# A planner with measured costs, and a second bank for the first heads' values, in an attention and two-MoE kernel

## The chip, the cores and the metric

The program runs on one core of one Trainium2 chip. The metric is the device time of one execution in microseconds; the median of the runs shown stands for the kernel. Every engine works through a list of instructions in order; what a list waits for is told by semaphores.

## The reference

Three stages follow each other on 2304 tokens (4 batches of 576) of width 512. First an attention with 8 heads of 64, causal, with a bias made from a running sum of `max(s, 0)`. Then a dense MoE-like layer (512 to 2048 to 512). Then a second one with eight experts (512 to 1024 to 512 each), whose weights per token come from eight rounds of row and column normalisation.

```python
scores = where(causal, -1e9, q @ k.T / 8 + minimum(-(cum_q - cum_k), 0))
attn = softmax(scores) @ v                      # 4 x 8 heads, 576 x 64
h = x @ w_in;  x = (h * sigmoid(1.702 * h)) @ w_out
P = balance(exp(x @ w_gate))                    # 8 rounds
out = sum_e P[:, e] * (relu(x @ w1[e]) @ w2[e])
```

All results are float32, and products are made from split numbers: a matrix product takes three fast ones (high by high, high by low, low by high).

## The kernel before, in words

Each of the 32 heads is handled in two parts, so that there are 64 "heads" in the code: the first 256 query rows (one unit, query blocks 0 and 1), and the other 320 (three units, blocks 2, 3 and 4). Eight parts of one kind make a group; the first group is n = 0 to 7. A unit passes four steps: `scores` (TensorE writes `sp`; VectorE adds the mask and takes the maximum into `sm`, a custom instruction with a read of its accumulator; ScalarE takes the exponential), `turn` (TensorE transposes `sm` into `tp`, which is copied to `pf`, or for n from 14 on split into `ph` and `pl`), `values` (TensorE multiplies with V into the tile `op`) and, when a head is whole, `finish` (VectorE divides: `stats`, reciprocal, `xg`).

PSUM has eight banks. Two hold the scores (tags S0 and S1), two the transposes (T0 and T1), one `op` (tag "O" of the pool `ps_a`), one `hp` (tag "h" of `ps_m`, first product of the first MoE), and two the sums of the first MoE (acc0 and acc1). As there is one bank for `op`, the values of head n wait until `finish` of head n-1 has read it.

The first MoE runs beside the attention, in blocks of 256 tokens and pairs of 128 hidden columns (`mm1`, `mm2`); a block can start when its heads are finished and its rows are transposed (`flush_x`). Its weights come as 64-bit words and are converted on the way (`conv`: two ScalarE passes, one VectorE pass into `t`, a copy to the high half `wih`/`woh`, a subtraction to the low half `wil`/`wol`). The last two blocks run together (`wide1`, `wide2`), and then the second MoE starts with its own planner mode (`seq.fine`).

The order of each engine's list is not written by hand. A `Sequencer` simulates the program while it is built: it gives each operation a cost, a time at which its operands are ready (the end of what it depends on plus a latency), and an end. TensorE's operations are issued at once, and its simulated clock, `free["PE"]`, is the time of the plan; operations of the other engines are held and issued when their simulated time comes, by rank (0 before 1 before 2; weight conversion has 2). The main loop asks in this order: vpow, flush, value, turn, score, first MoE. It takes the first that can start by the plan's time. Where none can, it moves the time itself:

```python
seq.free["PE"] = min(min(times), now + 100)
```

Work that two engines can do is given out by the plan too: `any_copy` takes VectorE or ScalarE, whichever has the lower load, `any_less` VectorE or GpSimd. All engines' rows carry L279, the line that records an operation.

Of the kernel before, what the change touches and what calls it, by code (L numbers as in the profile page):

```python
# [9 lines left out]
F32 = mybir.dt.float32  # L10
F32R = mybir.dt.float32r
# [22 lines left out]
BYTES = {F32: 4, F32R: 4, I32: 4, F16: 2, BF16: 2, U8: 1}  # L34
# [4 lines left out]
N_KF = 4  # L39
ADDING = 3.6  # L40
AFTER_OWN = 34
N_F = 14
NEXT_V = 11
LATE = 3000.0
# [5 lines left out]


class Op:
    __slots__ = ("engine", "call", "cost", "ready", "end", "waits", "after", "rank", "number", "nbytes", "late", "tail")


class Sequencer:
# [10 lines left out]
    def __init__(self):  # L67
        self.free = dict.fromkeys(self.ENGINES, 0.0)
        self.held = {e: [] for e in self.ENGINES}
        self.touched = {}  # L70
        self.earlier = {}
        self.rings = {}
        self.dma = self.issued = 0.0
        self.rank = 0
        self.holding = False
        self.fine = False
        self.late = 0.0
        self.count = 0
        self.outside = set()
# [50 lines left out]
    def cost(self, engine, what, out, ins, sums=False):  # L130
        n = max(self.size(x) for x in [out] + ins[:2])
        psum = any(x.space == PSUM for x in ins)
        if self.fine:
            if engine == "PE":
                return self.size(out) * (4 if ins[0].dtype == F32 else 1) / 2.4 + (13 if ins[0].dtype == F32R else 2.7)
            by = any(self.size(x) == 1 for x in ins[1:]) and n > 1
            if engine == "DVE":
                quick = what in ("tensor_copy", "tensor_scalar") and not psum
                return 66 + 60 * by + n / (1.92 if quick else 0.96)
            if engine == "ACT":  # L140
                return (50 if psum else 90) + 100 * by + 93 * sums + n / 1.2
        if engine == "PE":
            n = self.size(out)
            if what == "transpose":
                return 2 * n / 2.4
            slow = ins[0].dtype == F32 or ins[0].dtype == F32R and n < 256
            return n * (4 if slow else 1) / 2.4
        if engine == "DVE":
            quick = what in ("tensor_copy", "tensor_scalar") and not psum
            return 70 + n / (1.92 if quick else 0.96)  # L150
        if engine == "ACT":
            return 90 + n / 1.2
        return 80 + n * {"memset": 0.3, "tensor_scalar": 2.7}.get(what, 2.24)


    def submit(self, engine, what, call, outs, ins, adds=False):
        op = Op()
        op.engine, op.call, op.end, op.rank, op.number = engine, call, None, self.rank, self.count
        op.ready, op.waits, op.after, op.nbytes, op.tail = 0.0, set(), [], 0, 0
        op.late = self.late + (2000 if self.fine and self.rank else 0)  # L160
        self.count += 1
        if what == "dma_start":
            op.cost = 60 if engine == "SP" else 1000
            op.nbytes = self.size(outs[0]) * outs[0].shape[0] * (2 if self.fine and outs[0].dtype == F16 else 4)
            if adds and self.fine:
                op.nbytes *= ADDING
        else:
            sums = len(outs) > 1
            op.cost = self.cost(engine, what, outs[0], ins, sums) + (190 if sums and not self.fine else 0)
            if self.fine:  # L170
                op.tail = {"DVE": 85, "ACT": 110}.get(engine, 0) + 90 * sums
        for ap, writes in [(x, False) for x in ins] + [(x, True) for x in outs]:
            name = ap.tensor.name
            if name in self.outside:
                continue
            parts, cols = self.where(ap)
            mine = self.touched.setdefault(name, [])
            for x in self.touched.get(self.earlier.get(name), ()):
                self.depend(op, x[3])
            for x in mine:  # L180
                if (writes or x[2]) and x[3] is not op and not (ap.space == DRAM and writes and x[2]):
                    if x[0][0] < parts[1] and parts[0] < x[0][1] and x[1][0] < cols[1] and cols[0] < x[1][1]:
                        self.depend(op, x[3])
            mine[:] = [
                x for x in mine
                if x[3].end is None or x[3].engine != engine or x[2] != writes or x[0] != parts or x[1] != cols
            ]
            mine.append((parts, cols, writes, op))
        if engine == "PE" or not self.holding:
            self.issue(op)  # L190
        else:
            self.held[engine].append(op)

    def depend(self, op, on):
        if on.end is None:
            op.waits.add(on)
            on.after.append(op)
        elif self.fine and on.engine == op.engine != "PE" and not on.nbytes:
            op.ready = max(op.ready, on.end + AFTER_OWN)
        elif on.engine != "PE" or op.engine != "PE":  # L200
            op.ready = max(op.ready, on.end + LATENCY.get((on.engine, op.engine), LATENCY.get(on.engine, 0)))

    def issue(self, op):
        for x in sorted(op.waits, key=lambda x: x.number):
            if x.end is None:
                self.issue(x)
        e = op.engine
        start = max(self.free[e], op.ready)
        self.free[e] = start + op.cost
        op.end = start + op.cost + op.tail  # L210
        if op.nbytes:
            self.issued = max(self.issued, start) + 475
            self.dma = max(self.dma, self.issued + 1200) + op.nbytes / 360
            op.end = self.dma + 440 + op.late
        if op in self.held[e]:
            self.held[e].remove(op)
        op.call()
        op.call = None
        for x in op.after:
            x.waits.discard(op)  # L220
            self.depend(x, op)
        op.after = None

    def when(self, op):

# [95 lines left out]
def kernel(  # L321
# [12 lines left out]
    seq = Sequencer()  # L334
    nc = Core(seq, tc.nc)
    seq.outside |= {x.tensor.name for x in (qk, vP, s, w_in, w_out, wg, w1, w2, out)}
    B, H, D, S = qk.shape[0], qk.shape[1], qk.shape[2] // 2, qk.shape[3] // 2
# [45 lines left out]
    ps_m = Pool(seq, ctx.enter_context(tc.tile_pool(name="ps_m", bufs=1, space=PSUM, reuse_waits="tile")))  # L383
    ps_a = Pool(seq, pa.enter_context(tc.tile_pool(name="ps_a", bufs=1, space=PSUM, reuse_waits="tile")))
# [30 lines left out]
    stats = apool.tile([128, 14], F32, name="stats")  # L415
# [133 lines left out]
    begin = []  # L549
# [283 lines left out]
    def turn(i):  # L833
# [21 lines left out]
        )  # L855
        live[i] = (ph, pl, blocks, spots)

    def values(i):
        n, u = units[i]
        qb0 = extent(n)[6][0]  # L860
        v3 = v3_of[n]
        ph, pl, blocks, spots = live.pop(i)
        if u[0] == qb0:
            outs[n] = (
                ps_a.tile([128, 3, D + 1], F32, tag="O", name="op"), stats[:, 8 + n % 2 * 3:11 + n % 2 * 3]
            )
        op, den = outs[n]
        for m, (qb, rows, ke, a) in enumerate(blocks):
            mine = [x for x in spots if x[0] == qb]
            o = op[:rows, qb - qb0, :]  # L870
            for w, (_, kb, _, at) in enumerate(mine):
                if n < N_F:
                    nc.tensor.matmul(
                        o, lhsT=ph[:, at:at + rows], rhs=v3[kb], start=(w == 0), stop=(w == len(mine) - 1)
                    )
                    continue
                for part, nv in ((ph, 2), (pl, 1)):
                    for j in range(nv):
                        v = v3[j][:, kb, :]
                        nc.tensor.matmul(  # L880
                            o[:, 0:v.shape[1]], lhsT=part[:, at:at + rows], rhs=v,
                            start=(w == 0 and part is ph and j == 0),
                            stop=(w == len(mine) - 1 and part is pl and j == nv - 1),
                        )
# [81 lines left out]
    def can_value():  # L966
        if n_v >= n_t or units[n_v][0] not in v3_of:
            return never
        n, u = units[n_v]
        if n > n_fin:  # L970
            return never
        x = [live[n_v][0], live[n_v][1], *v3_of[n]]
        return max([seq.slot(ps_a, "O") if n not in outs else 0] + [seq.settled(a.tensor.name) for a in x])

    def do_value():
        nonlocal n_v
# [1197 lines left out]
    turn_, count, idle, hooked, over = 0, 0, 0, 0, {}  # L2174
# [86 lines left out]
```

## Time and profile before

| what | value |
|---|---|
| median of 3 runs | 1993.34 us (1993.1 to 1995.27) |
| the profiled execution | 1995.91 us |
| its span, first to last instruction | 1994.1 us |
| mean granted TensorE clock | 0.998 |
| busy: TensorE, VectorE, ScalarE, GpSimd | 98%, 72%, 62%, 17% |

Busy time of TensorE counts pipelined matmuls from their start to a modelled end, so that it hides short waits; the distance from one start to the next says more. The attention and most of the first MoE lie in the first 570 us, the wide blocks from there to 655 us, the second MoE behind it.

### The profile page before, as it was taken

What the parts mean: (1) busy time and instruction counts of PE and PEld (TensorE: products, weight loads), DVE (VectorE), ACT (ScalarE), POOL (GpSimd) and SP (SyncE); (2) the same over time, 40 slices, a digit from 0 to 9 for tenths busy, and PEclk for the clock granted to TensorE, in tenths of its full rate; (3) what the DMA queues carried; (4) which work ended last, traced back from release to release, by engine and by line L of the source; (5) the groups of instructions that cost most, each with busy time, mean ns of one, the idle gap of its engine ahead of it and who ended that gap; (6) DMA issues with size and microseconds to landing.
All of it is one profiled execution on the core that took longest, in us unless ns stands there. A gap on an engine that the chain in (4) does not pass through costs nothing.

```text
span 1994.1 us, 41095 instructions
## 1 busy us (share of the span) xinstructions
PE 1956.2 (98%) x15683; PEld 1575.5 (79%) x15683; DVE 1427.6 (72%) x3240; ACT 1227.5 (62%) x2525; POOL 335.0 (17%) x376
## 2 busy tenths in 40 slices
PE   6999999999999999999999999999999999999999
PEld 5889999999988677777777777777777777777777
DVE  5886776776743776887877767776787776776656
ACT  4776765766643665665666666656666666565343
POOL 3565444443300000000000011111100001111000
PEclk9999999999999999999999999999999999999999
DMA  7555444454335544565484565666648556566331
GB/s 221 159 178 181 138 131 138 129 146 116 86 94 186 208 152 146 202 232 182 147 273 133 153 186 156 172 197 184 167 120 261 147 150 186 156 172 183 119 130 43
DMA packets 230100, 322.11 MB, mean 162 GB/s; under 512 B 38272, under 2 KB 156224, under 8 KB 229904
## 3 DMA queue, kind: packets, MB, share of 16 engines
q1 hardware_dynamic: 216944, 295.90, 45.2%
q0 software_dynamic: 12960, 23.60, 8.2%
q8 instruction: 123, 2.02, 0.4%
q14 instruction: 73, 0.60, 0.1%
HBM read 230.85 MB, written 84.34 MB: 158 GB/s over the span
## 4 chain that ended last, share of the span: by engine, by line
PE 81%; DVE 9%; ACT 6%; DMA 2%; issue 1%; SPq 0%; POOL 0%; ACTq 0%; DVEq 0%
PE C L279 16%; PE A L279 16%; PE D L279 16%; PE hp L279 8%; PE B L279 8%; PE acc L279 5%; PE op L279 3%; PE sp L279 3%; PE tp L279 2%; ACT h L279 2%; PE accw L279 2%; DVE h L279 2%; DVE t L279 1%; DVE hst L279 1%; PE accx L279 1%
## 5 line engine op out<-in xcount | busy, mean ns | idle before, releaser
L279 PEld LDWEIGHTS <-h 128*128 128x128 f16 x6048 | 591.3, 98 | 86.3 <-issue 7.6
L279 PEld LDWEIGHTS <-w1o 128*128 128x128 f16 x4036 | 394.6, 98 | 255.1 <-issue 4.5
L279 POOL DMA_DIRECT2D acc_d<-y x90 | 77.8, 865 | 1186.5 <-DVE y L279 662.1
L279 PE MATMUL C<-xt,w1o 128*128 128x384 f16 x1152 | 218.6, 326 | 1.4 <-DVE hst L279 1.4
L279 PE MATMUL D<-xt,w1o 128*128 128x384 f16 x1152 | 218.4, 326 | 0.0
L279 PE MATMUL D<-w2o,h 128*128 128x256 f16 x1728 | 217.7, 273 | 0.2 <-ACT y L279 0.2
L279 PE MATMUL A<-xt,w1o 128*128 128x384 f16 x1152 | 214.8, 326 | 0.1
L279 PE MATMUL A<-w2o,h 128*128 128x256 f16 x1728 | 212.2, 273 | 1.7 <-ACT B L279 1.4
L279 PE MATMUL C<-w2o,h 128*128 128x256 f16 x1728 | 208.4, 273 | 2.5 <-DVE y L279 1.7
L279 DVE SCALAR_TENSOR_TENSOR h<-hst,h 128x768 f16<-128x768 f32 (+1 forms) x192 | 139.1, 755 | 55.9 <-ACT h L279 55.9
L279 ACT COPY C<-B 128x384 f32<-128x384 f32 (+1 forms) x168 | 71.5, 426 | 153.8 <-PE B L279 92.7
L279 PE MATMUL hp<-xh,wih 128*128 128x256 f32 (+1 forms) x512 | 154.4, 302 | 1.3 <-DVE t L279 0.7
L279 PE MATMUL hp<-xl,wih 128*128 128x256 f32 (+1 forms) x512 | 152.0, 297 | 0.0
L279 PE MATMUL hp<-xh,wil 128*128 128x256 f32 (+1 forms) x512 | 151.8, 297 | 0.0
L279 ACT ACTIVATE h<-hst 128x768 f16<-128x768 f32 (+1 forms) x192 | 126.2, 678 | 3.8 <-DVE hst L279 3.8
L279 ACT ACTIVATE sm<-sm,stats 64x576 f32<-64x576 f32 (+4 forms) x160 | 94.5, 600 | 34.0 <-DVE stats L279 33.7
L279 PE MATMUL acc<-gh,woh 128*128 128x256 f32 x384 | 110.9, 289 | 0.0
L279 PE MATMUL B<-w2o,h 128*128 128x256 f16 x864 | 110.5, 273 | 0.1
L279 PE MATMUL B<-xt,w1o 128*128 128x384 f16 x576 | 109.3, 326 | 0.0
L279 PE MATMUL acc<-gl,woh 128*128 128x256 f32 x384 | 108.5, 282 | 0.0
L279 PE MATMUL acc<-gh,wol 128*128 128x256 f32 x384 | 108.3, 282 | 0.0
L279 ACT COPY B<-A 128x384 f32<-128x384 f32 (+1 forms) x168 | 70.2, 425 | 58.4 <-PE A L279 57.6
(242 smaller groups left out, 4041.8 us busy)
## 6 DMA issues: line engine op xcount, KB each, us to landing
xt<-xc_d SPq DMA_DIRECT2D x168, 384.0 KB
wm<-in_moe_w_dram SPq DMA_DIRECT2D x112, 256.0 KB
w2o<-w_d SPq DMA_DIRECT2D x56, 512.0 KB
wr<-in_moe_w_dram SPq DMA_DIRECT2D x112, 256.0 KB
w_d<-wo SPq DMA_DIRECT2D x98, 256.0 KB
acc_d<-y POOLq DMA_DIRECT2D x90, 256.0 KB, 4.8
kq<-in_qk_dram SPq DMA_DIRECT2D x32, 448.0 KB
st<-in_moe_w_in_dram SPq DMA_DIRECT2D x16, 512.0 KB
```

Of the source, the lines that this page charges most:

```text
L279: self.seq.submit(self.name, what, lambda: method(*args, **named), outs, ins, "accum_op" in named)
```

## The change

Two things. First, the costs that the planner used in its fine mode for the second MoE are now used for the stages before it too: per-instruction floors and surcharges for VectorE and ScalarE, the tails between an instruction's issue and its result (85 and 110 ns, 90 more with an accumulator), 34 ns instead of a whole latency between two dependent instructions of one engine, and 13 or 2.7 ns more for a matmul. A new method, `array`, adds the part of a weight load that the matmul before does not cover, and doubles TensorE's times while `cold` is set. Second, `values` puts `op` of the odd heads below 8 into the first MoE's bank acc0 instead of bank O.

```diff
+WARM = 6300
@@ Sequencer.__init__
+        self.cold, self.since, self.streamed = True, 0.0, 0.0
@@ cost
-            if engine == "DVE":   # (and ACT: in the fine mode alone)
         if engine == "PE":
             n = self.size(out)
             if what == "transpose":
-                return 2 * n / 2.4
+                return 2 * n / 2.4 + 3
-            return n * (4 if slow else 1) / 2.4
+            return n * (4 if slow else 1) / 2.4 + (13 if ins[0].dtype == F32R else 2.7)
+        by = any(self.size(x) == 1 for x in ins[1:]) and n > 1
         if engine == "DVE":
-            return 70 + n / (1.92 if quick else 0.96)
+            return 66 + 60 * by + n / (1.92 if quick else 0.96)
         if engine == "ACT":
-            return 90 + n / 1.2
+            return (50 if psum else 90) + 100 * by + 93 * sums + n / 1.2
@@ submit
-            op.cost = self.cost(engine, what, outs[0], ins, sums) + (190 if sums and not self.fine else 0)
-            if self.fine:
-                op.tail = {"DVE": 85, "ACT": 110}.get(engine, 0) + 90 * sums
+            if engine == "PE":
+                op.load = 110 if BYTES[ins[0].dtype] == 4 else 27
+            op.cost = self.cost(engine, what, outs[0], ins, sums)
+            op.tail = {"DVE": 85, "ACT": 110}.get(engine, 0) + 90 * sums
@@ depend
-        elif self.fine and on.engine == op.engine != "PE" and not on.nbytes:
+        elif on.engine == op.engine != "PE" and not on.nbytes:
             op.ready = max(op.ready, on.end + AFTER_OWN)
@@ issue
         start = max(self.free[e], op.ready)
+        if e == "PE" and not self.fine:
+            start = self.array(op, start)
+    def array(self, op, start):
+        idle = start > self.free["PE"] + 50
+        if idle:
+            self.since = start
+        if start - self.since > WARM:
+            self.cold = False
+        by = 2 if self.cold else 1
+        op.cost *= by
+        begin = start + max(0.0, by * op.load - (0.0 if idle else self.streamed))
+        self.streamed = op.cost
+        return begin
@@ values, and the slot that can_value asks for
+    def o_of(n):
+        return (ps_m, "acc0") if n < H and n % 2 else (ps_a, "O")
```

## Rows read from the trace of the kernel before

**Rows 1.** The page: busy time of the engines, and the chain that ended last.
```profile
PE 1956.2 (98%) x15683; PEld 1575.5 (79%) x15683; DVE 1427.6 (72%) x3240; ACT 1227.5 (62%) x2525; POOL 335.0 (17%) x376
...
PE 81%; DVE 9%; ACT 6%; DMA 2%; issue 1%; SPq 0%; POOL 0%; ACTq 0%; DVEq 0%
```

**Rows 2.** Windows: stretch in us, its length, busy us and instructions per engine, clock, DMA.
```profile
0.00:50.00 50.00, 34.07 (x134) 28.33 (x134) 29.84 (x103) 22.40 (x44) 16.82 (x32) 1.00 0.74 221
50.00:170.00 120.00, 112.01 (x992) 104.40 (x992) 103.72 (x261) 92.60 (x178) 72.60 (x69) 0.97 0.53 169
170.00:570.00 400.00, 396.25 (x3904) 380.21 (x3903) 282.68 (x842) 258.29 (x528) 167.77 (x186) 1.00 0.45 129
655.00:1994.00 1339.00, 1328.83 (x10286) 992.65 (x10285) 976.68 (x1931) 821.30 (x1705) 77.81 (x90) 1.00 0.57 170
```

**Rows 3.** Timeline of TensorE: start, duration, what, [idle before it, ended by].
```profile
8.67 4.18 PE L279 MATMUL sp<-kf 66*128 66x128 f32 x12 [8.67 <-DMA kf<-aux]
...
17.55 2.90 PE L279 MATMUL sp<-kf 66*128 66x128 f32 x8 [0.33 <-DMA kf<-in_qk_dram]
...
24.60 1.51 PE L279 MATMUL op<-vf,pf 128*128 128x65 f32 x6 [0.79 <-DVE xg L279]
25.91 0.84 PE L279 MATMUL tp<-ident,sm 128*128 128x128 f32 x3
...
28.83 1.51 PE L279 MATMUL op<-vf,pf 128*128 128x65 f32 x6 [0.80 <-DVE xg L279]
...
32.76 0.37 PE L279 MATMUL vtp<-ident,vmax 128*2 128x128 f32 x1 [1.78 <-DVE vmax L279]
...
36.24 1.51 PE L279 MATMUL op<-vf,pf 128*128 128x65 f32 x6 [1.13 <-DVE xg L279]
...
41.54 1.52 PE L279 MATMUL op<-vf,pf 128*128 128x65 f32 x6 [2.44 <-DVE xg L279]
42.82 0.67 PE L279 MATMUL sp<-one 128*128 128x384 f32 x1
...
44.60 1.51 PE L279 MATMUL op<-vf,pf 128*128 128x65 f32 x6
...
49.49 0.78 PE L279 MATMUL op<-vf,pf 128*128 128x65 f32 x6
...
55.30 0.36 PE L279 MATMUL hp<-xh,wih 128*128 128x256 f32 x1
```

**Rows 4.** The chain in order of time, before the second group: start, length, what.
```profile
26.45 4.00 DMA kq<-in_qk_dram
```

**Rows 5.** Timeline of VectorE: two score reductions, and the second group's first copy.
```profile
10.45 0.29 DVE L279 CUSTOM_DVE_ANT_0 sm<-sp,mask 128x128 f32<-128x128 f32 x1 [4.87 <-PE sp L279]
...
10.67 0.42 DVE L279 CUSTOM_DVE_ANT_0 sm<-sp,mask 128x256 f32<-128x256 f32 x1
...
34.59 0.62 DVE L279 CAST one<-kq 128x896 fp32r<-128x896 f32 x1
```

**Rows 6.** Windows of one microsecond around the fall of the clock.
```profile
113.00:114.00 1.00, 0.35 (x4) 0.12 (x2) 0.96 (x4) 1.00 (x4) 0.92 (x2) 0.98 1.01 344
114.00:115.00 1.00, 1.00 (x12) 0.94 (x13) 1.00 (x3) 0.87 (x3) 0.92 (x2) 0.50 0.85 298
...
120.00:121.00 1.00, 1.00 (x13) 0.91 (x13) 0.29 (x1) 1.00 (x4) 0.41 (x3) 0.61 0.97 317
```

**Rows 7.** Groups, 50 to 170 us: busy us, mean ns: ScalarE's exponentials, a VectorE copy.
```profile
L279 ACT ACTIVATE sm<-sm,stats 128x256 f32<-128x256 f32 x8 | 4.0, 500 | 0.0
...
L279 DVE CAST woh<-t 128x512 fp32r<-128x512 f32 x10 | 7.0, 696 | 0.1
```

**Rows 8.** Instructions on the tile sm, 50 to 170 us: duration ns min/median/max, first and last start.
```profile
L279 ACT ACTIVATE sm<-sm,stats x37: 386/615/778, 50.2 to 162.5; 128x128 f32<-128x128 f32 x8, 128x256 f32<-128x256 f32 x8, 128x384 f32<-128x384 f32 x7, 128x512 f32<-128x512 f32 x7
L279 DVE CUSTOM_DVE_ANT_0 sm<-sp,mask x36: 275/444/692, 50.9 to 159.8; 128x128 f32<-128x128 f32 x8, 128x256 f32<-128x256 f32 x8, 128x512 f32<-128x512 f32 x7, 64x288 f32<-64x288 f32 x7
...
L279 DVE CUSTOM_DVE_ANT_0 sm<-sp,mask,stats x7: 478/499/503, 54.8 to 104.3; 64x288 f32<-64x288 f32 x7
```

More of the change, by code (lines that the diff above doesn't have):

```diff
@@ L52 @@
 class Op:
-    __slots__ = ("engine", "call", "cost", "ready", "end", "waits", "after", "rank", "number", "nbytes", "late", "tail")
+    __slots__ = ("engine", "call", "cost", "ready", "end", "waits", "after", "rank", "number", "nbytes", "late", "tail", "load")
 class Sequencer:
@@ L135, in cost @@
                 return self.size(out) * (4 if ins[0].dtype == F32 else 1) / 2.4 + (13 if ins[0].dtype == F32R else 2.7)
-            by = any(self.size(x) == 1 for x in ins[1:]) and n > 1
-            if engine == "DVE":
[L138 to L141, printed above, removed]
         if engine == "PE":
@@ L158, in submit @@
         op.engine, op.call, op.end, op.rank, op.number = engine, call, None, self.rank, self.count
-        op.ready, op.waits, op.after, op.nbytes, op.tail = 0.0, set(), [], 0, 0
+        op.ready, op.waits, op.after, op.nbytes, op.tail, op.load = 0.0, set(), [], 0, 0, 0
         op.late = self.late + (2000 if self.fine and self.rank else 0)
@@ L863, in values @@
         if u[0] == qb0:
+            pool, tag = o_of(n)
             outs[n] = (
-                ps_a.tile([128, 3, D + 1], F32, tag="O", name="op"), stats[:, 8 + n % 2 * 3:11 + n % 2 * 3]
+                pool.tile([128, 3, D + 1], F32, tag=tag, name="op"), stats[:, 8 + n % 2 * 3:11 + n % 2 * 3]
             )
@@ L972, in can_value @@
         x = [live[n_v][0], live[n_v][1], *v3_of[n]]
-        return max([seq.slot(ps_a, "O") if n not in outs else 0] + [seq.settled(a.tensor.name) for a in x])
+        return max([seq.slot(*o_of(n)) if n not in outs else 0] + [seq.settled(a.tensor.name) for a in x])
     def do_value():
```

## The prediction

> **What bounds the kernel now.** I read the page first. TensorE is busy 98% of the span and carries 81% of the chain that ended last [rows 1], so time is won or lost where TensorE waits or runs slowly. The windows say where that is [rows 2]. From 655 us on it is busy 1328.8 of 1339 us, from 170 to 570 it lacks 3.75 us, from 50 to 170 us 8.0, and in the first 50 us 15.9. All that the change can reach lies before 570 us; the second MoE's own costs stay as they are.
>
> The third view is TensorE's timeline of the beginning [rows 3]. It starts at 8.67 us, when the first operands land. Then it waits 0.79, 0.80, 1.13 and 2.44 us, each time with `op` and each time for `xg`: the one bank of `op` is not yet read. These are 5.16 us. One more wait of 1.78 us is for `vmax`.
>
> The same rows hold a second loss. Six records of `op` last 1.51 us at 24.60 and 0.78 us at 49.49. [...] Before the rise it had run without a gap from 41.54 us, 7.5 us long; the run from 17.55 to the wait that ended at 24.60 was 6.3 us long and brought no rise. Between 8.67 and 49 us it worked some 33 us (40.3 less 7.27 us of waits), at half speed.
>
> The clock falls once more. After a stretch in which TensorE was busy 35% of a microsecond the granted clock is 0.50 from 114 us to about 120.6 [rows 6]; 6.6 us at half speed cost up to 3.3 us.
>
> **The change part by part.** All sums are made against the profiled execution, 1995.91 us (span 1994.1 and 1.8 around it). It is 2.6 us above the median of the runs, 1993.34, and I subtract these 2.6 at the end.
>
> *The bank.* Heads 1, 3, 5 and 7 no longer wait for the reading of the head before them; a head waits for the one two places back. No instruction is added, and acc0 has no other user then: its first sum needs the first token block, thus all eight heads. The four waits of 5.16 us can go. What is late next is the second group: `kq` lands at 30.45 [rows 4], its first copy runs on VectorE at 34.59 [rows 5], and its first scores start at 42.82 [rows 3]. In VectorE's list that copy stands behind the first group's reductions and divisions, which follow TensorE. So part of what TensorE gains it may spend waiting there. Bounds: 0 and -5.2 us; I take -4, near the rows, because the first MoE's `hp` (at 55.30, after the first block is finished) comes earlier too and can fill.
>
> [...]
>
> *The halved clock in the plan.* This part does nearly nothing, which the planner's own constants show. The plan's first scores need `aux0`: its source lands at 475 + 1200 + 147456/360 + 440 = 2525 ns; with the new costs three VectorE operations follow (199 + 85, 34 + 333 + 85, 34 + 333 + 85), then 128, 475, 1200, 11 and 440 ns for the small DMA, and 200 in `settled`: 6167 ns. `since` is 0 until an idle stretch is seen, and none is seen, because the main loop has moved `free["PE"]` up to that very time. 6167 is under 6300, so the first matmul is doubled (220 ns of load, 432 of work); the second starts at 6819, and `cold` is off for good. So the plan runs TensorE at full speed while the chip runs at half until the rise. I count 0 for it, with bounds of -1 and +1 us.
>
> *The clock on the chip.* With the four waits gone, TensorE can run without a gap from 17.55 us on. The rise might come at about 25 us in place of 49; then some 16 us of work at half speed would take 8 (23.5 us less 6.94 of waits, halved). Or new waits for VectorE break the run, and it comes as late as before. Bounds 0 and -8; I take -1.5, near the row at 24.60, where 6.3 us were not enough, for the second group's data break any run around 35 us.
>
> *The costs of VectorE and ScalarE.* They now agree with the rows. Two score reductions start 0.22 us apart [rows 5]; the plan had 70 + 133 + 190 = 393 ns and now has 199. An exponential of 256 columns lasts 0.50 us with its tail [rows 7]; the plan had 303 ns and now has 403 + 110. A result of VectorE or ScalarE is now planned 85 to 110 ns later, so TensorE's list will come to it less often too early. What can be won are the waits of 8.0 and 3.75 us from 50 to 570 us [rows 2] and the 3.3 us of the fallen clock. What can be lost is the balance (the third rival). Bounds -15 and +9; I take -2.5, a sixth of what lies there, since no row shows which waits a new order meets.
>
> *The matmul costs.* The first MoE's matmuls are planned at 120 ns and not 107, so the plan's time stretches by an eighth, and DMA issues and conversions stand earlier in TensorE's terms. I count 0, bounds -1 and +1; their loads had cover already, for from 170 to 570 us TensorE lacks under 1% [rows 2].
>
> *The second MoE* starts earlier by what was won, with the same costs: 0, bounds -1 and +1.
>
> The sum: -4 + 0 - 1.5 - 2.5 = -8.0, thus 1987.9 us for the profiled execution, and **1985.3 us** beside the median of 1993.34; I say 1985.
>
> **The rivals.**
>
> *The waits move.* TensorE reaches the second group's scores earlier and waits there, the first MoE's block waits for its weights, the clock rises as late as before, and from 50 to 170 us VectorE, busy 103.7 of 120 us [rows 2], sets the pace. For it: `kq` lands at 30.45 whatever TensorE does. Against it: 12.4 us pass from there to the first scores at 42.82, and most of this is lists that stood still behind `op`. The costs -2.5 and 1.5 us of new waits leave 1992.
>
> *The clock rises early.* If no new gap comes, the -8 stand in place of the -1.5, the fall at 114 us does not come back (-3.3 more), and the sum is -17.8: 1975.5. For it: for each head TensorE has some 3.3 us of work at half speed (1.4 for the scores, as 4.18 serve three heads; 0.6 to 0.8 for the transposes at 25.91; 1.3, from 24.60 to 25.91, for `op` [rows 3]), more than VectorE needs for the same head (0.6 for the two reductions [rows 5], and by the planner's new costs 0.8 for copy and division). Against it: VectorE has the conversions as well, and the second group comes around 35 us.
>
> [...]
>
> *Slower: copies go to VectorE.* `any_copy` gives a copy to the engine with the lower planned load. From 50 to 170 us the trace holds 36 + 7 score reductions and 37 exponentials [rows 8]; the new costs take 43 x 0.194 = 8.3 us off VectorE's planned load and put 3.7 us on ScalarE's. So copies go over to VectorE, where one of 512 columns takes 0.70 us on average [rows 7, 8]. If half of the 12 us of shifted load goes over, that is 6 us or some 9 copies; VectorE has 16.3 us free in this stretch [rows 2], and part of that is waits for TensorE's results. It decides from the point where VectorE reaches 95% (114 us), that is if 15 or more go over: 10 us more work in its list, of which TensorE sees some 6 beyond what was won, and a second fall of the clock (3.3) with it. If in addition only half of the bank's gain stays, the sum is 10 + 3.3 - 2 - 1.5 = +9.8, and the time 2003.
>
> **How the numbers follow.** A difference of 0.2%, 4 us, is about what a measurement of this kernel can tell from none. The forecast, 1980 to 1989.3, has 0.46; the early clock, below 1980, 0.14; the waits that move, 1989.3 to 1997.3, 0.21; the slower case 0.19. So faster has 0.60, the same 0.21, slower 0.19. The range from 1974 to 2000 leaves out about a third of the early clock's chance and two thirds of the slower one's, under 0.2 together. The bounds of single terms added up would reach further on both sides, but they do not all come together.
>
> **What would show it.** In the changed kernel's TensorE timeline no `op` below head 8 should wait for `xg`; the six records of the last such `op` should start by 40 us and not 44.60; `hp` should start by 48 us and not 55.30. The durations of `op` tell when the clock rose. From 50 to 170 us VectorE's busy time should stay under 106 us; 110 or more would speak for the slower case. The first wide block should start 6 to 10 us earlier, and the second MoE's length should stay within 1 us. It would be wrong if TensorE's waits from 50 to 570 us grow by more than 8 us, or if the gaps before 50 us only change their names.

## The result, and the profile after

The changed kernel takes 2013.28 us (median of 4 runs, 2012.44 to 2016.27) against 1993.79 beside it: a ratio of 1.0098 [1.0085, 1.0111], 19.5 us slower. I had said 1985, with 2000 as the upper end. The profiled execution took 2016.27 us against 1995.91, its span 2014.2 against 1994.1. The page first, busy time and chain of waits:

```profile
PE 1963.0 (97%) x15683; PEld 1578.2 (78%) x15683; DVE 1432.9 (71%) x3259; ACT 1219.1 (61%) x2505; POOL 335.6 (17%) x377
...
PE 74%; DVE 11%; ACT 6%; DMA 5%; issue 2%; POOL 2%; SPq 1%; ACTq 0%; DVEq 0%; POOLq 0%
```

The work is the same; TensorE's share of the chain fell from 81% to 74%, and VectorE, DMAs and GpSimd took it [rows 1]. The windows say where, in the columns of [rows 2]:

```profile
0.00:50.00 50.00, 36.01 (x159) 31.91 (x159) 34.20 (x106) 24.14 (x47) 18.21 (x33) 1.00 0.77 226
50.00:170.00 120.00, 110.22 (x974) 102.50 (x973) 104.39 (x278) 89.99 (x172) 76.54 (x72) 0.97 0.58 181
170.00:570.00 400.00, 381.88 (x3729) 360.68 (x3728) 276.01 (x830) 242.91 (x496) 159.10 (x180) 1.00 0.43 122
655.00:1994.00 1339.00, 1332.84 (x10225) 995.09 (x10224) 976.25 (x1926) 826.94 (x1712) 77.88 (x90) 1.00 0.56 168
```

From 170 to 570 us TensorE lacked 3.75 us before and lacks 18.1 now. That was the stretch where I saw nothing to lose. From 50 to 170 us it lacks 9.8 instead of 8.0; in the first 50 us it is busy 1.9 us longer. The first wide block, which ends this half of the kernel, gives the sum, before and after (count, then duration in ns: least, median, most; then first and last start):

```profile
L279 PE MATMUL accw<-gh,woh x64: 388/389/397, 573.5 to 654.8; 128*128 128x512 f32 x64
L292 PE MATMUL accw<-gh,woh x64: 388/389/397, 594.7 to 676.0; 128*128 128x512 f32 x64
```

It starts 21.2 us later, which is as large as the whole loss (20.4 us between the two profiled executions). Up to it TensorE stands idle 41.9 us (594.7 less 552.8 busy) and stood 27.7: 14.2 more. The other 7.0 are longer busy time for the same 5040 matmuls. Of these some 1.7 are a second fall of the clock (3.4 us at a granted clock of 0.50, below); busy time also counts the whole record of the last matmul before a wait (0.28 us for an `hp` of 256 columns), where one in a row adds 0.12 (310.70 to 310.82 us). Counted from start to start at full clock, the 45 distances with a recorded wait in them are 35.2 us longer together than the median distance of their kind of matmul (before 19 and 13.5 us); all the others are 18.9 us too long, and were 19.5. So the loss is waiting, not slower matmuls.

The beginning went nearly as I said. TensorE's timeline:

```profile
24.46 1.38 PE L292 MATMUL op<-vf,pf 128*128 128x65 f32 x6
...
30.01 1.53 PE L292 MATMUL op<-vf,pf 128*128 128x65 f32 x6
...
32.27 2.79 PE L292 MATMUL op<-vf,pf 128*128 128x65 f32 x12
...
35.07 0.84 PE L292 MATMUL xtp<-ident,xg 128*128 128x128 f32 x3
37.63 1.33 PE L292 MATMUL xtp<-ident,xg 128*128 128x128 f32 x5 [1.73 <-DVE vw L292]
...
42.41 0.58 PE L292 MATMUL vbp<-vd,ones_b 2*128 2x4 f32 x2 [3.45 <-DVE xl L292]
42.93 0.69 PE L292 MATMUL sp<-one 128*128 128x384 f32 x1
...
44.59 0.41 PE L292 MATMUL hp<-xh,wih 128*128 128x256 f32 x1
...
46.08 0.41 PE L292 MATMUL hp<-xl,wih 128*128 128x256 f32 x1
46.30 0.33 PE L292 MATMUL hp<-xh,wil 128*128 128x256 f32 x1
46.46 0.28 PE L292 MATMUL hp<-xh,wih 128*128 128x256 f32 x1
```

No `op` of the first eight heads waits for `xg` any more; the last of them end at 35.1 us, where they ended at 46.1 [rows 3]. But the second group's first scores start at 42.93 us and started at 42.82. Part of what TensorE gained it spends waiting at `xtp` and `vbp` (1.73 and 3.45 us); another part the earlier `hp` (44.59, not 55.30) fills. The step from 0.41 to 0.28 us at 46.3 is the rise of the clock. In the kernel before it came 2.7 us later, at about 49 us, between the records of six `op` with 1.51 us at 44.60 and with 0.78 at 49.49 [rows 3].

The clock also falls, in the rows of [rows 6]: at 107.8 us (it was 114.0), and, which it did not do before, at 435.5 us for 3.4 us:

```profile
107.00:108.00 1.00, 0.00 (x1) 0.03 (x2) 1.00 (x7) 0.84 (x3) 0.92 (x2) 0.91 0.20 48
108.00:109.00 1.00, 1.00 (x13) 0.91 (x14) 1.00 (x4) 1.00 (x3) 1.00 (x1) 0.50 0.00 0
114.00:115.00 1.00, 1.00 (x17) 0.94 (x15) 0.25 (x3) 0.30 (x1) 0.93 (x3) 0.68 0.90 253
435.00:436.00 1.00, 1.00 (x9) 1.00 (x8) 0.07 (x1) 0.00 (x0) 0.76 (x1) 0.75 0.19 12
438.00:439.00 1.00, 1.00 (x7) 1.00 (x7) 0.27 (x1) 0.30 (x1) 0.60 (x1) 0.54 0.81 244
```

What TensorE waits for from 170 to 570 us, the five largest (who, for whom: us in all, times, longest):

```profile
PE hp L292 <- DVE t L292: 5.1, 5, 1.9
PE op L292 <- DVE pl L292: 3.5, 8, 0.9
PE sp L292 <- DVE stats L292: 2.3, 3, 1.8
PE tp L292 <- DVE xl L292: 2.1, 2, 1.2
PE vbp L292 <- DVE pl L292: 1.5, 1, 1.5
```

It waits for VectorE, though VectorE is busy only 276 of 400 us; so it can matter what stands ahead of the awaited instruction in VectorE's list. One such wait, the scores at 312.97 us, first on TensorE, then on VectorE and on GpSimd:

```profile
310.94 0.28 PE L292 MATMUL hp<-xh,wil 128*128 128x256 f32 x1
312.97 0.35 PE L292 MATMUL sp<-one 128*64 128x288 f32 x1 [1.76 <-DVE stats L292]
```

```profile
309.93 1.40 DVE L292 TENSOR_TENSOR wa<-wa,wb 128x256 f32<-128x256 f32 x1
311.25 0.67 DVE L292 TENSOR_REDUCE xmx<-xo 128x1 f32<-128x512 f32 x1
...
311.91 0.47 DVE L292 SCALAR_TENSOR_TENSOR wb<-wa,early,wb 128x256 f16<-128x256 f32 x1
...
312.38 0.53 DVE L292 CUSTOM_DVE_ANT_0 sm<-sp,mask 128x384 f32<-128x384 f32 x1
312.84 0.08 DVE L292 DVE_READ_ACCUMULATOR2_ANT stats<- 128x1 f32 x1
```

```profile
309.63 1.42 POOL L292 TENSOR_TENSOR gl<-t,gh 128x512 fp32r<-128x512 f32 x1 [1.54 <-ACT gh L292]
```

Ahead of the reduction for which the scores wait stand `wa` and `wb`, preparation of the second MoE's weights that nobody needs yet. `wa` is planned with 66 + 256 / 0.96 = 333 ns and a tail of 85, that is 418 to its result, and its median here is 426: the plan has the usual one right, but this one takes 1.40 us while GpSimd runs. Of the 21 waits over 0.25 us in this stretch (16.7 us in all) 15, with 12.9 us, end with a VectorE instruction that had such preparation (`wa`, `wb`, `xa`, `xb`) among the five before it; of all VectorE's other instructions in the stretch 37% had. Before it was 4 of 6 waits, 2.8 of 3.75 us.

### The profile page after: what moved, and what is told of

The parts are those of the page before. It is cut to its first block, busy times and chain, and to the rows that moved or that the text cites. A ratio compares the mean times of both kernels' runs of the same rounds, so it can differ in the third digit from the quotient of the medians.

```text
span 2014.2 us, 41058 instructions
## 1 busy us (share of the span) xinstructions
PE 1963.0 (97%) x15683; PEld 1578.2 (78%) x15683; DVE 1432.9 (71%) x3259; ACT 1219.1 (61%) x2505; POOL 335.6 (17%) x377
## 4 chain that ended last, share of the span: by engine, by line
PE 74%; DVE 11%; ACT 6%; DMA 5%; issue 2%; POOL 2%; SPq 1%; ACTq 0%; DVEq 0%; POOLq 0%
PE C L292 16%; PE A L292 16%; PE D L292 16%; PE B L292 8%; PE hp L292 6%; PE acc L292 3%; ACT h L292 2%; PE accw L292 2%; PE op L292 2%; DVE h L292 2%; PE sp L292 2%; PE tp L292 1%; DMA kq<-in_qk_dram 1%; DVE sm L292 1%; DVE t L292 1%
## 5 line engine op out<-in xcount | busy, mean ns | idle before, releaser
L292 DVE SCALAR_TENSOR_TENSOR t<-t,hp 128x512 f32<-128x512 f32 x72 | 49.1, 682 | 87.1 <-ACT t L292 87.1
```

Source lines behind the costliest of these rows:

```text
L292: self.seq.submit(self.name, what, lambda: method(*args, **named), outs, ins, "accum_op" in named)
```

## The experiments

Ratios are against the kernel before, on the same chip; the runs are from several chips, on which the kernel before has medians of 1993.8 to 1995.7 us, so rows are compared by their ratios. "Idle" is TensorE's, the length of the window less its busy time; the last column is when the first wide block starts; both are from the profiled execution.

| run | median us | ratio [95%] | idle 50–170 | idle 170–570 | wide from |
|---|---|---|---|---|---|
| before | 1993.8 | 1 | 8.0 | 3.8 | 573.5 |
| e11, e9, e10: VectorE, TensorE latency +2, GpSimd +2 ns | 1996.1, 1998.2, 2000.1 | 1.0009 [0.9999, 1.0018], 1.0018 [1.0009, 1.0027], 1.0027 [1.0017, 1.0038] | 6.6, 9.0, 10.8 | 3.6, 1.9, 3.9 | 572.7, 575.2, 575.7 |
| e1: bank alone | 1997.1 | 1.0018 [1.0008, 1.0027] | 10.9 | 2.7 | 575.0 |
| e15: before, matmuls x 0.93 | 1997.9 | 1.0015 [1.0006, 1.0025] | 7.1 | 1.1 | 573.4 |
| e6: before, reductions -190 ns | 1999.5 | 1.0027 [1.0017, 1.0036] | 8.1 | 6.4 | 578.1 |
| e4: after, old TensorE costs | 2007.9 | 1.0062 [1.0047, 1.0077] | 11.3 | 3.9 | 581.5 |
| e7, e8: after, VectorE x 1.14, 1.3 | 2004.9, 2007.8 | 1.0051 [1.0034, 1.0068], 1.0065 [1.0048, 1.0083] | 11.0, 14.4 | 10.9, 8.3 | 582.7, 583.6 |
| e18, e17: e5, DMAs or other engines x 1.12 | 2010.5, 2011.7 | 1.0076 [1.0061, 1.0091], 1.0080 [1.0063, 1.0098] | 13.3, 7.4 | 7.7, 9.1 | 588.9, 586.7 |
| e5: before, new TensorE costs | 2012.4 | 1.0089 [1.0074, 1.0104] | 9.9 | 10.5 | 590.1 |
| e16: before, half of them | 2015.5 | 1.0105 [1.0090, 1.0120] | 8.5 | 11.2 | 590.6 |
| after | 2013.3 | 1.0098 [1.0085, 1.0111] | 9.8 | 18.1 | 594.7 |
| e12: after, TensorE latency +2 ns | 2015.9 | 1.0109 [1.0094, 1.0124] | 9.5 | 16.9 | 592.5 |
| e2: after without the bank | 2019.8 | 1.0123 [1.0108, 1.0139] | 11.4 | 12.9 | 598.5 |
| e13, e14: after, 300, 600 ns more reserve | 2020.8, 2025.2 | 1.0133 [1.0118, 1.0148], 1.0151 [1.0134, 1.0168] | 13.8, 15.7 | 15.2, 17.6 | 599.8, 606.3 |
| e3: after without the halved clock | 2024.3 | 1.0147 [1.0132, 1.0162] | 13.8 | 15.6 | 601.4 |

**The parts apart.** The bank alone: `o_of` put into the kernel before. Then the costs without the bank, and the costs without the halved clock:

```
# e2
-        return (ps_m, "acc0") if n < H and n % 2 else (ps_a, "O")
+        return (ps_a, "O")
# e3
-        self.cold, self.since, self.streamed = True, 0.0, 0.0
+        self.cold, self.since, self.streamed = False, 0.0, 0.0
```

> The kernel before with nothing but the second bank for the first heads; all old costs stay. Reserve theory (the old costs were wrong in TensorE's favour's opposite: they planned its matmuls at 107 ns where they take 120, and the score reductions 0.19 us too long, so operands were there early; the new costs take this reserve away and TensorE comes too early): 1986 to 1993, the gain of the beginning alone. Bank theory (the bank changes the order of the beginning and all that follows is worse): 2008 or more. Order theory (any small shift of the plan gives another order, whose time is a lot drawn): anywhere from 1985 to 2012.

> The changed kernel with the old single bank; all new costs stay. Reserve theory: 2010 to 2020, the whole loss and some 3 us more for the waits of the beginning. Bank theory: 1990 to 1996. Order theory: anywhere from 1990 to 2020.

> The changed kernel with the halved clock never applied in the plan (cold starts as false). In the plan only the first matmul was doubled, a shift of 0.65 us. Reserve theory: 2008 to 2018, as the changed kernel. Order theory: this shift is a new lot, so a time that differs by more than 5 us from the changed kernel's 2013 either way. If the halved clock in the plan matters by itself: slower than 2018 without it.

The loss is in the costs (e2), not in the bank. The bank alone wins nothing (with the new costs, after against e2, it goes with 0.25%): what e1 gains at the start it gives back from 50 to 200 us, where other waits stand than before (3.2 and 2.7 us; before 2.6 and none), e1's rows:

```profile
PE op L279 <- DVE pl L279: 3.2, 3, 1.5
PE tp L279 <- ACT sm L279: 2.7, 3, 1.3
```

e3 is 0.49% (10 us) slower than after: the halved clock doubles only the plan's first matmul, but that shifts what follows, and the list comes out otherwise. So a small difference says nothing until it is known what an arbitrary list is worth.

**TensorE's costs taken out, and alone.**

```
# e4 (the call of self.array in issue is left out too)
-                return 2 * n / 2.4 + 3
+                return 2 * n / 2.4
-            return n * (4 if slow else 1) / 2.4 + (13 if ins[0].dtype == F32R else 2.7)
+            return n * (4 if slow else 1) / 2.4
# e5: the two old returns of before replaced by the two new ones, nothing else
```

> The changed kernel with TensorE's old costs (107 ns for a matmul of 256 columns, no loads, no halved clock); VectorE's and ScalarE's new costs and the bank stay. Reserve theory: 12% of TensorE's time is planned away again, so operands are there earlier: 1990 to 2003, and TensorE's waits from 170 to 570 us fall from 18 to under 10 us. Copies theory (copies that went to VectorE load it): 2008 or more, since the balance stays. Bank theory: 2008 or more.

> The kernel before with TensorE's new matmul costs alone (13 or 2.7 ns more, transposes 3); no loads, no halved clock, no bank, VectorE and ScalarE as before. Reserve theory (what TensorE's low costs planned away was time for its operands to arrive): slower by itself, 2000 to 2012, with TensorE's waits from 200 to 600 us up by 8 us or more. If the loss needs VectorE's new costs: within 5 us of 1993.

The windows of e4, then of e5:

```profile
50.00:170.00 120.00, 108.74 (x930) 100.92 (x928) 104.49 (x265) 82.55 (x156) 69.40 (x68) 0.94 0.51 162
170.00:570.00 400.00, 396.09 (x3895) 377.46 (x3894) 297.97 (x855) 255.48 (x520) 167.94 (x187) 1.00 0.45 129
```

```profile
50.00:170.00 120.00, 110.07 (x975) 102.38 (x975) 102.93 (x272) 94.16 (x182) 76.11 (x72) 0.97 0.57 179
170.00:570.00 400.00, 389.53 (x3798) 369.71 (x3797) 273.84 (x830) 247.40 (x501) 160.18 (x179) 1.00 0.43 124
```

Thirteen ns on each F32R matmul (and 2.7 or 3 on the others) in the planner, nothing else, cost 0.89%, 17.7 us: nearly the whole loss. The new cost is nearer to the trace: one `hp` of 256 columns starts 0.12 us after another, where the plan had 107 ns and now has 120. But the waits are not the same ones. From 170 to 570 us the largest in e5 is that of `op` for the division before it, in the kernel after that of `hp` for VectorE's reading of its bank, 5.1 us; e5's row:

```profile
PE op L279 <- DVE xg L279: 4.9, 7, 1.4
```

With the old costs e4 has its 170 to 570 us back (3.9 us idle). Its own loss lies before: 3.3 us more idle from 50 to 170, and a mean clock of 0.94 and not 0.97, which over 120 us is 3.6 more. That is about the 7.2 us of its profiled execution (2003.13); its median lies 4.8 us above that one, and no trace shows why. The two effects do not add up: 17.7 us (0.89%) and 12.4 (0.62%) against 19.5 for both.

**VectorE's costs.** `e6` takes the 190 ns from VectorE's score reductions in the kernel before; `e7` and `e8` raise VectorE's costs up to the second MoE in the kernel after.

```
# e6
+            ... + (190 if sums and not self.fine and engine == 'ACT' else 0)
# e7 (e8: 1.3)
+            return (1 if self.fine else 1.14) * (66 + 60 * by + n / (1.92 if quick else 0.96))
```

> The kernel before with the 190 ns taken off VectorE's score reductions in the plan, and nothing else. Reserve theory: 32 us of VectorE's planned time from 50 to 570 us go, so PE comes earlier to its operands: 1998 to 2010, with the growth from 50 to 200 us where the score reductions are dense. Copies theory (VectorE seems less loaded and gets more copies): the same time, but then VectorE's busy time from 50 to 170 us rises above 108 us (103.7 before). Neither: within 4 us of 1993.

> The changed kernel with VectorE's planned costs of the first stages raised by 14%, to the sum that the trace of the changed kernel shows for 50 to 590 us (361 us against 317 planned). If the plan only has to be true on the mean: 1990 to 2000. If it needs a reserve for TensorE above the truth: some better than 2013, 2000 to 2010. Order theory: 2005 to 2025.

> As the last, with 30%: VectorE planned 15% slower than it is. If the plan only has to be true on the mean: worse than with 14%, by 5 us or more. Reserve theory: as good as with 14% or better, 1988 to 2003, with TensorE's waits from 200 to 600 us near those of the kernel before.

e7 gets 0.47% back, 9.4 of the 19.5 us, and the intervals of e7 and after lie apart; e8 gets no more. So VectorE's costs, 14% too low in the kernel after by the expectation of e7 (361 us in the trace against 317), may be up to half of the loss, give or take what one list differs from another (below); but TensorE's idle time from 170 to 570 us stays at 10.9 and 8.3.

**What an arbitrary list is worth.** One constant moved by 2 ns, in before three times (`"PE": 199`; `return 82 + n *` for GpSimd; `"DVE": 130`) and once in after (`"PE": 199`):

> The kernel before with one constant of the plan moved by 2 ns (TensorE to others: 199 for 197), which gives another order of all engines and changes no estimate in earnest. Cost theory (what the plan believes of TensorE and VectorE makes the loss): within 5 us of 1994. Chosen-order theory (the order of before is the best of many lots, and any new lot is worse): 2000 to 2012.

> The kernel before with GpSimd's fixed cost at 82 for 80 ns, another lot of the same kind. Cost theory: within 5 us of 1994. Chosen-order theory: 2000 to 2012.

> The kernel before with VectorE's latency at 130 for 128 ns, a third lot. Cost theory: within 5 us of 1994. Chosen-order theory: 2000 to 2012.

> The changed kernel with TensorE's latency at 199 for 197 ns, a second lot of the new costs beside the run without the halved clock (2024). Cost theory: 2008 to 2026, above every lot of the old costs. Chosen-order theory: the lots of the old and of the new costs overlap, so anything from 1998 to 2026.

Two nanoseconds without a meaning cost 0.09 to 0.27% (1.8 to 5.4 us), of which e11's 0.09 can't be told from nothing: the kernel before is at or near the best of these four lists, which the expectations call lots. Against the mean of the other three (1.0018) the change costs 0.80%, 16 us and not 19.5, and e1, e6 and e15 can't be told from a lot. The lists with the new costs scatter more: after, e12 and e3 stand at 1.0098, 1.0109 and 1.0147. None of these, nor e2 at 1.0123, comes near the lots of the old costs. So the loss is not just that the new list is another one.

**More reserve.** If the list comes too early to data that come late, more distance should help: `settled`, the time from which the planner takes a result as there, moved by 300 and 600 ns more (`x[3].end + (200 if self.fine else 500)`, `800`):

> The changed kernel, where TensorE may begin a piece of work only 500 ns (200 before) after the planned end of what it reads or overwrites, in the first stages. Costs are as in the changed kernel. Reserve theory (operands must be there early, by whatever means): much of the loss comes back, 1996 to 2008, TensorE's waits from 170 to 570 us under 12 us (18 in the changed kernel). Rate theory (the true speed of TensorE lets the plan put too much other work between, and only the ratio of the speeds helps): 2010 to 2022.

> As the last with 800 ns. Reserve theory: as good or better, 1994 to 2008, unless the plan itself now idles. Rate theory: 2010 to 2025.

It does not: the ratio rises by 0.35 and 0.53% (7 and 10.6 us), e13 within what e12 and e3 scatter, e14 at its upper edge. The reserve theory falls. Part of this rise may be the clock: between its first rise and the wide block TensorE has a granted clock of 0.50 for 10.2 us in the kernel after, 17.1 in e13 and 27.3 in e14 (before 6.8); from 50 to 170 us the mean clock is 0.97, 0.94 and 0.92 (before 0.97). At 0.50 up to half of the time is lost, so of e14's 10.6 us up to 8.5 may be this.

**The size of the error.** TensorE planned 7% faster than before (`/ 2.4 * 0.93`), and half of the new addition (`+ (6.5 if ins[0].dtype == F32R else 2.7)`):

> The kernel before with TensorE's planned matmuls 7% shorter still (99 ns where 120 are true; transposes as before). Reserve theory: at least as good as other orders of the old costs, 1990 to 2000. If the old costs just happened to be right for the balance: 2003 or more.

> The kernel before with half of the new surcharge on TensorE's split matmuls (6.5 for 13 ns, 2.7 for the others; transposes as before). If the loss grows with the planned cost, between the orders of the old costs (1994 to 2000) and the full surcharge (2012): 2000 to 2008. If it sits on a threshold: either 1994 to 2000 or 2009 to 2015.

Planned further from the chip, TensorE loses nothing that a lot does not lose; planned half way nearer, it loses all. So the loss does not grow with the size of the change. Of the twelve lists with higher TensorE costs none is under 1.0051; of the eight with the old or lower ones seven are at 1.0027 or under, and e4 is at 1.0062. Lower costs were tried once, in e15.

**The ratio to the others.** Perhaps the old plan was right because all engines were planned too fast by about the same part. Then e5 with the others raised by 12% as well should be as fast as before: VectorE, ScalarE and GpSimd (`return 1.12 * (70 + n / ...)`, `1.12 * (90 + n / 1.2)`, `213` for `190`) or the DMAs (`475 * by`, `1200 * by`, `op.nbytes / 360 * by`, `440 * by`, with `by = 1 if self.fine else 1.12`):

> The kernel with TensorE's new matmul costs alone (2012), and VectorE, ScalarE and GpSimd planned 12% slower in the first stages, so that the ratio of the engines is again that of the kernel before (a matmul of 256 columns 120 for 107 ns is the same 12%). Rate theory (it is the ratio of TensorE's planned speed to the other engines' that decides, since it says how much of their work goes between two matmuls): the order and the time of the old costs, 1993 to 2002. If the ratio to the DMAs decides, or any new order is bad: 2008 or more.

> The kernel with TensorE's new matmul costs alone (2012), and the DMAs planned 12% slower, the engines as in that kernel. Rate theory with the engines: 2006 to 2018, no help. If the ratio to the DMAs decides: 1993 to 2002.

Neither can be told from e5, so at 12% both ratio theories fall. Here is the group that stands in TensorE's way, the second MoE's `wb`, on VectorE, after and then in e17:

```profile
L292 DVE SCALAR_TENSOR_TENSOR wb<-wa,early,wb x48: 457/481/1374, 199.0 to 358.0; 128x256 f16<-128x256 f32 x48
```

```profile
L279 DVE SCALAR_TENSOR_TENSOR wb<-wa,early,wb x48: 447/484/1648, 221.3 to 408.5; 128x256 f16<-128x256 f32 x48
```

Before the 48 ran from 210.5 to 420.0 us. After has them in 159 us and not 210, so VectorE's list is denser with them; the wait at 312.97 us shows how that can hold TensorE up. But e17 spreads them over 187 us and is as slow, and e7 has them from 196 to 358 and is faster. Density alone doesn't set the time. Nor is this preparation behind the waits of every slow list: in e3, slower than after, 5 of the 13 waits that VectorE ends had it among the five instructions before (3.8 of 11.2 us), which is no more than its share of VectorE's list. A list with this filler capped was not tried.

**What stays open.** Shown: TensorE's truer costs alone bring nearly the whole loss, and in every list with them or with half of the addition TensorE's idle time from 170 to 570 us is 7.7 to 18.1 us, in every one with the old costs 1.1 to 6.4. Read from the trace and not tested: that the preparation ahead of urgent reductions in VectorE's list is a path by which they do it, in after and in e5 (9 of the 11 waits that VectorE ends there, 6.1 of 7.0 us); e3 speaks against its being the only one. Not explained: why the planner's order gets worse at all when TensorE's costs are truer, why half of the addition does as much as all of it, and why e4 loses 12.4 us with no new TensorE cost at all. None of the lists is faster than before.

## Why the prediction was wrong

**The step that failed** is the matmul costs: "I count 0, bounds -1 and +1; their loads had cover already, for from 170 to 570 us TensorE lacks under 1%". They measured +17.7 us alone (e5). In the stretch on which the argument rested TensorE lacks 10.5 us there and 18.1 in the kernel after, where it lacked 3.75. I looked only at what the stretching of the plan does to loads and conversions. But the order of all the engines' lists hangs on TensorE's planned clock. One reading, not tested, is that with more planned time per matmul the planner finds more room on VectorE and hands out filler earlier than it is needed; why the new order is worse stays open. That the stretch had hardly a gap meant that it had little to win; I read it as nothing to lose. These are the two sides of a bound, and I priced one.

**VectorE's and ScalarE's costs**, -2.5 with +9 as the upper bound: wrong in sign. With TensorE's old costs (e4) the ratio is 1.0062, +12.4 us (the bank's part is in it), beyond the bound. The reductions alone (e6) cost what a lot costs. "They now agree with the rows" was no argument: the list isn't better because its costs are.

**The bank**, -4: the four waits went, as said. By 50 us 2.7 us are gained; by 200 us they are given back, and the bank alone stands at 1.0018 [1.0008, 1.0027]. "What is late next" was the right question with the right answer (the second group's data, 42.93 us against 42.82), and the price, a quarter of the gain, was too low.

**The clock on the chip**, -1.5: the rise came 2.7 us earlier, worth half of that by the two `op` durations, 1.51 and 0.78 us; then 1.7 were lost again to a second fall. The early rise fell although its condition held: TensorE ran without a gap from 8.71 to 35.9 us. That some 7.5 us of work without a gap bring the rise, on which a rise at 25 us rested, no run shows: 7.5 us came before it in the kernel before, but there 8.5 us from 8.67 on [rows 3], and here these 27 us, brought none.

**The halved clock in the plan** reaches one matmul by the working. That does not make its removal free: e3's list is another one, and worse by 0.49%. **The second MoE** kept its length: from the first wide block to the end 1420.6 us before, 1419.5 after.

**The rivals.** The slower one had the right side and the wrong mechanism: its time, 2003, is 10 us short, VectorE is busy 104.4 us from 50 to 170, under the 106 I had set, and most of the loss lies from 170 to 570. The waits that move did so in the first 200 us, but without the gain that this rival kept. The test that I set for being wrong, waits from 50 to 570 us that grow by more than 8 us, was met: 11.75 to 27.9.

**The range.** My bounds added up to +12 at most on the upper side, under the 19.5 measured, and the unknown order of a whole list stood in it as sizes of single costs. Three lists with a 2 ns shift would have shown that a list scatters upwards by up to 5.4 us. That alone would not have reached 19.5; the rest is the matmul costs' term, with a bound of +1.

## What to carry to other kernels

A list made by a planner is a draw: before a change of its costs is judged, time a few lists with a meaningless shift (here +0.1 to +0.3%), and change one cost at a time. A cost that is truer by itself can make a worse list; where an engine takes filler in order, look at what stands ahead of the instruction that the bounding engine waits for. An engine with hardly a gap has little to win from a new order, and here it stood idle 14.4 us longer in such a stretch.

## What the hardware showed beside this

TensorE worked without a gap from 8.71 to 35.9 us, 27 us of fp32 scores, values and transposes, and stayed at the lower of the two speeds that its records show (six `op` records take 1.38 us at 24.46 and 1.53 at 30.01; in the kernel before 0.78 after the rise, at 49.49 [rows 3]); the rise came at 46.3 us, after a gap and 3.9 us of `vbp`, scores and `hp`. In the row of the first 50 us the granted clock stands at 1.00.

VectorE's longest instructions run beside GpSimd. From 170 to 570 us, 35 of VectorE's instructions before and 32 after last over 0.3 us longer than the median of their tile and operation, 23.9 and 22.5 us in all; each of them runs beside a GpSimd instruction for more than half of its time, which 42 and 38% of all VectorE's instructions there do. The `wa` of 1.40 us above is one. Since the sums are alike, it is not the slowing that differs; who waits behind it may.
